# Pooled attention with a token and channel mixer: tail copies from SBUF, and the last tail maxima in the second bank of the AV result tile

## The chip, the cores and the metric

The kernel runs on one core of one Trainium2 chip. The metric is the device time of one execution in microseconds. Three timed runs of the kernel before gave 1417.49, 1419.48 and 1420.95 us; the median, 1419.48 us, is the figure to compare with. One further execution was profiled, and it took 1416.78 us; its trace spans 1414.8 us.

## The reference

For 8 batches and 8 heads, queries are pooled in pairs (1152 rows become 576), scored against 1152 keys, put through a softmax with its row maximum subtracted, and multiplied with the values. The result goes through a mixer: an angle, two token matrices, a channel matrix.

```python
q_pool = q.reshape(B, H, S // 2, 2, D).mean(axis=3)          # 8, 8, 576, 64
scores = np.matmul(q_pool, k.transpose(0, 1, 3, 2)) / np.sqrt(D)
scores = scores - np.max(scores, axis=-1, keepdims=True)
attn = np.exp(scores)
attn = attn / (np.sum(attn, axis=-1, keepdims=True) + 1e-09)
x = np.matmul(attn, v)                                       # -> 8, 576, 512
theta = x @ w_theta
zr, zi = x * np.cos(theta), x * np.sin(theta)
u = x + einsum('ts,bsd->btd', w_tok_r, zr) + einsum('ts,bsd->btd', w_tok_i, zi)
out = u + np.maximum(u @ w_ch, 0.0)
```

## The kernel before

The attention is the first stage (until about 932 us of the span), the mixer the second. The change lies in the first alone.

The unit of the attention is a **pair** of heads, numbered i = 0 to 31. The two heads lie in the two halves of the 128 partitions. For each pair, keys and pooled queries are turned by TensorE into a PSUM tile `pt` in two groups (g = 0: six key blocks; g = 1: six query blocks and three key blocks). ScalarE rounds each into the SBUF tile `hi` (L281), VectorE writes the remainder into `lo` (L292).

The **row maxima** of the scores are worked out ahead of the scores. 512 of a pair's 576 queries per head take 12 passes (`maxpass`, L305 on TensorE and L312 on VectorE). The last 64 queries of both heads, the *tail*, are packed by two ScalarE copies (`prep_tail`, L288) into one block-diagonal 128x128 tile, and `max_tail` multiplies it with all 1152 keys: 1024 of them into a tile `px` (L322, reduced by L331), the last 128 into a free corner of the `pt` of a later pair (L328, reduced by L332). The maxima of a pair are gathered into one row per head (`max_row`: a TensorE transpose into the tile `pmt`, copied by L344, sent by DMA) and enter the scores as a further matmul.

The **scores** of a pair are 18 steps (2 query halves u by 9 key blocks kt): eight matmuls into a tile `pe` (L371), one exponential on ScalarE into `pc` (L374), and a running sum on GpSimd (L383).

The **AV** product of a half u runs as one burst of 18 groups of matmuls, `av` (L392), into a tile `pa`, which ScalarE then copies out (L399). The rest of the work is put around the two bursts of a pair:

- the burst of u = 0 of pair i: `prep_all(i + 2, 1)`, then `max_row(i + 1)`, then `av(i, 0)`, then the sums of pair i - 1 (`norm_sum`, L408, in the `pmt` tile that L344 reads);
- the burst of u = 1 of pair i: `tail_prep(i)`, which turns group 0 of pair i + 3 and works out the tail maxima of pair i + 2, then `av(i, 1)`.

PSUM is used in **double tiles** of two banks (2 x 512 words per partition), in two rings of two: ring "e" holds `pe` and `pa`, ring "m" holds `pt`, `px`, `pmt` and `pm`. `pa` uses only columns 0 to 287 of its first bank. The order on every engine is written out by hand: each piece has a place on one scale of positions (`at`), the pieces are sorted by it, and each engine runs its instructions in just that order. Semaphore waits are put in between by a framework that follows which instruction writes and reads which tile.

Beside the attention, VectorE, ScalarE and GpSimd convert the mixer's weights piece by piece (L525 to L555).

Of the kernel before, what the change touches and what calls it, by code (L numbers as in the profile page):

```python
# [9 lines left out]
F32 = mybir.dt.float32  # L10
# [4 lines left out]
ALU = mybir.AluOpType  # L15
AX = mybir.AxisListType
# [75 lines left out]
def pooled_attention_moe_kernel(  # L92
# [11 lines left out]
    nc = tc.nc  # L104
    P = 128
    B, H, S, D = k.shape
    SQ = S // 2
    DM = H * D
    HALF = SQ // 2
    HT = SQ % P  # L110
# [3 lines left out]
    QP = SQ // QT  # L114
    NP = H // 2
    NPAIR = B * NP
# [31 lines left out]
    def bank2(kind, name):  # L148
        return psum["now"][0].tile([P, 2, 512], F32, tag=kind, name=name, bufs=PAIRS[kind])
# [38 lines left out]
    with ExitStack() as p1:  # L188
# [21 lines left out]
        state = {}  # L210
# [32 lines left out]
        def prep(i):  # L243
            st = state[i]
            for n in ("hi", "lo"):
                st[n] = opd.tile([P, SQ + S], F32R, tag=n, name=f"{n}{i}")
            st["nmr"] = nmrs[i % 2]

        K0 = {t: SQ * (t >= 6) + t * P for t in range(KT)}
        Q0 = 6 * P  # L250

        def prep_t(i, g):
            st = state[i]
            kn = st["kn"]
            pt = st["pt", g] = bank2("m", f"pt{g}_{i}")
            if g == 0:
                srcs = [[kn[:, t] for t in range(3 * n, 3 * n + 3)] for n in range(2)]
            else:
                qp = st["qp"]
                srcs = [[qp[:, t] for t in range(5)], [qp[:, 5]] + [kn[:, t] for t in (6, 7, 8)]]  # L260
            for n in range(2):
                c = 0
                for src in srcs[n]:
                    R = src.shape[0]
                    nc.tensor.transpose(  # L265
                        out=pt[:, n, c : c + R],
                        in_=src.rearrange("p h d -> p (h d)"),
                        identity=ident[0:R, 0:R],
                    )
                    c += R  # L270

        def prep_parts(i, g):
            st = state[i]
            c0, w = ((0, 3 * P), (Q0, 5 * QP))[g]
            return st["pt", g][:, :, 0:w], *(
                st[n][:, c0 : c0 + 2 * w].rearrange("p (b c) -> p b c", b=2) for n in ("hi", "lo")
            )

        def prep_hi(i, g):
            src, hi, lo = prep_parts(i, g)  # L280
            nc.scalar.copy(hi, src)  # L281

        def prep_tail(i):
            st = state[i]
            tl = st["tail"] = tails[i % 2]
            c = QP - HT
            for hs in HEADS:
                nc.scalar.copy(tl[hs, hs], st["pt", 1][hs, 1, c : c + HT])  # L288

        def prep_lo(i, g):  # L290
            src, hi, lo = prep_parts(i, g)
            nc.vector.tensor_tensor(lo, src, hi.bitcast(F32), ALU.subtract)  # L292
# [24 lines left out]
        def max_tail(i, pt):  # L317
            st = state[i]
            hi, tl, mx = st["hi"], st["tail"], st["mx"]
            pm = bank2("m", f"px{i}")  # L320
            for n, c, k, w in ((0, 0, 0, 4), (1, 0, 4, 2), (1, 2 * P, 6, 2)):
                nc.tensor.matmul(  # L322
                    pm[:, n, c : c + w * P], tl, hi[:, K0[k] : K0[k] + w * P], start=True, stop=True
                )
            st["pm", 0] = pm
            if pt is None:
                pt = bank2("m", f"py{i}")
            nc.tensor.matmul(  # L328
                pt[:, 0, 3 * P :], tl, hi[:, K0[8] : K0[8] + P], start=True, stop=True
            )  # L330
            nc.vector.tensor_reduce(mx[:, 8, 0:2], pm, AX.X, ALU.max)  # L331
            nc.vector.tensor_reduce(mx[:, 8, 2:3], pt[:, 0, 3 * P :], AX.X, ALU.max)  # L332

        def max_nm(i):
            st = state[i]
# [3 lines left out]
        def max_row(i):  # L339
            st = state[i]  # L340
            px = bank2("m", f"pmt{i}")
            nc.tensor.transpose(out=px[0:KT, 0, 0:P], in_=st["nm"], identity=ident)
            mT = st["mT"] = sml.tile([KT, P], F32R, tag="mT", name=f"mT{i}")
            nc.scalar.copy(mT, px[0:KT, 0, 0:P])  # L344
            return px
# [36 lines left out]
            first = st["pc"][u, 0] if kt == 1 else st["ss", u]  # L382
            nc.gpsimd.tensor_tensor(st["ss", u], first, st["pc"][u, kt], ALU.add)  # L383

        def av(i, u):
            st = state[i]
            if u == 0:
                st["xu"] = nrm.tile([P, 2, HALF], F32, tag="xu", name=f"xu{i}", bufs=3)
            pa = bank2("e", f"pa{i}_{u}")
            for kt in range(KT):  # L390
                for h, hs in enumerate(HEADS):
                    nc.tensor.matmul(  # L392
                        pa[hs, 0, 0:HALF],
                        st["vn"][:, h, kt, :],
                        st["pc"][u, kt][:, h, :],
                        start=(kt == 0),
                        stop=(kt == KT - 1),
                    )
            nc.scalar.copy(st["xu"][:, u, :], pa[:, 0, 0:HALF])  # L399

        def norm_sum(i, px):
            st = state[i]
            sets = [[st["ss", u]] + [st["pc"][u, kt] for kt in range(TAIL, KT)] for u in range(2)]
            for n in range(len(sets[0])):
                for h in range(2):
                    for u in range(2):
                        a = 32 * (2 * h + u)
                        nc.tensor.matmul(  # L408
                            px[a : a + 32, 1, 0:HALF],
                            ones,  # L410
                            sets[u][n][:, h, :],
                            start=(n == 0),
                            stop=(n == len(sets[0]) - 1),
                            tile_position=(0, a),
                        )
            sm = st["sm"] = sml.tile([P, HALF], F32, tag="sm", name=f"sm{i}", bufs=1)
            nc.scalar.activation(sm, px[:, 1, 0:HALF], AF.Identity, bias=eps)
# [38 lines left out]
        def burst(i, u):  # L456
            if u == 0:
                if i + 2 < NPAIR:
                    prep_all(i + 2, 1)
                px = max_row(i + 1) if i + 1 < NPAIR else bank2("m", f"pmt{i}")  # L460
                av(i, u)
                if i > 0:
                    norm_sum(i - 1, px)
            else:
                tail_prep(i)
                av(i, u)

        def prep_all(i, g):
            if g == 0:
                prep(i)  # L470
            prep_t(i, g)
            prep_hi(i, g)
            prep_lo(i, g)
            if g == 1:
                prep_tail(i)

        def tail_prep(i):
            more = i + 3 < NPAIR
            if more:
                prep(i + 3)  # L480
                prep_t(i + 3, 0)
            if i + 2 < NPAIR:
                max_tail(i + 2, state[i + 3]["pt", 0] if more else None)
            if more:
                prep_hi(i + 3, 0)
                prep_lo(i + 3, 0)

        def norm_store(i):
            b, hp = divmod(i, NP)
# [158 lines left out]
        def plan(i):  # L648
# [7 lines left out]
            if i < 2:  # L656
                at(PRO[i][1], 3, prep_all, i, 1)
                at(PRO[i][2], 3, max_tail, i, None)
# [12 lines left out]
            for u in range(2):  # L671
                at(base + AV_AT[u], 4, burst, i, u)
# [318 lines left out]
```

## Time and profile before

| | |
|---|---|
| timed runs, median | 1419.48 us (1417.49 to 1420.95, 3 runs) |
| profiled execution, own time | 1416.78 us |
| its span | 1414.8 us, mean granted TensorE clock 0.992 |
| busy share of the span | PE 96%, weight load 77%, GpSimd 64%, VectorE 61%, ScalarE 52% |
| DMA | 111.66 MB, 79 GB/s on average |

The profile's rows give, for an instruction, its start in us from the span's start, its length in us, engine, line, operation, output and inputs; in square brackets stands how long the engine was idle before it and what ended that. PE is TensorE's matmul, PEld its weight load, DVE VectorE, ACT ScalarE, POOL GpSimd. In the view of stretches, the column PEclk is the granted clock as a share of the full one, and the number behind an engine's busy time is its count of instructions.

### The profile page before, as it was taken

How to read it: one execution, taken by the hardware profiler on the slowest of the kernel's cores; microseconds unless marked ns; L12 is line 12 of the kernel's file. 1: busy time of each engine (PE TensorE's matmuls, PEld its weight loads, DVE VectorE, ACT ScalarE, POOL GpSimd, SP SyncE). 2: the span in 40 equal slices, each digit the busy share in tenths (PEclk: the TensorE clock that was granted, in tenths of full speed). 3: DMA queues.
4: the chain of work that ended last, by engine and by line, in shares of the span. 5: the costliest groups of instructions: out<-in, count | busy, mean ns of one | idle time of the engine just before them, and what ended most of it. 6: DMA issues, size and time to landing. Idle time of an engine off the chain costs nothing.

```text
span 1414.8 us, 29922 instructions
## 1 busy us (share of the span) xinstructions
PE 1352.8 (96%) x12178; PEld 1086.1 (77%) x12178; DVE 862.2 (61%) x1143; ACT 730.6 (52%) x1250; POOL 911.4 (64%) x672
## 2 busy tenths in 40 slices
PE   5999999999999999999999999999999999999998
PEld 4667676766676767767776766688999999999998
DVE  5866676777577767766687666355362553536442
ACT  2556465655555655556565655465444544445431
POOL 2789888978798889889898888834232413232210
PEclk7999999999999999999999999999999999999999
DMA  5224343434342443324343421231111211111111
GB/s 127 74 75 126 85 111 84 119 85 116 86 125 69 108 122 106 94 83 125 84 111 86 119 80 51 79 122 38 35 38 34 60 50 34 38 35 44 28 31 38
DMA packets 130906, 111.66 MB, mean 79 GB/s; under 512 B 95040, under 2 KB 95424, under 8 KB 130768
## 3 DMA queue, kind: packets, MB, share of 16 engines
q1 hardware_dynamic: 130592, 109.28, 28.0%
q8 instruction: 96, 1.57, 0.5%
q0 software_dynamic: 176, 0.46, 0.1%
q14 instruction: 42, 0.34, 0.1%
HBM read 88.29 MB, written 21.27 MB: 77 GB/s over the span
## 4 chain that ended last, share of the span: by engine, by line
PE 67%; DVE 15%; ACT 10%; DMA 3%; issue 3%; POOL 1%; SPq 0%; ACTq 0%; POOLq 0%; DVEq 0%
PE pa L392 16%; PE pe L371 16%; PE py L821 11%; PE pth L743 7%; PE pr L860 5%; DVE mx L312 5%; ACT pc L374 4%; PE pm L305 3%; PE pt L265 3%; PE pmt L408 2%; DMA kn<-in_k_dram 2%; DVE wf L532 1%; PE pxn L731 1%; DVE ws L530 1%; DVE lo L292 1%
## 5 line engine op out<-in xcount | busy, mean ns | idle before, releaser
L383 POOL TENSOR_TENSOR ss<-ss,pc 128x576 f32<-128x576 f32 x384 | 558.1, 1453 | 98.2 <-ACT pc L374 75.9
L312 DVE TENSOR_REDUCE mx<-pm 128x2 f32<-128x768 f32 x384 | 343.9, 950 | 134.8 <-PE pm L305 134.4
L374 ACT ACTIVATE pc<-pe 128x576 f32<-128x576 f32 x576 | 371.2, 652 | 102.2 <-PE pe L371 84.2
L392 PE MATMUL pa<-pc,vn 128*64 128x288 f32 x2304 | 293.5, 409 | 0.3 <-ACT pc L374 0.3
L794 POOL TENSOR_TENSOR Z<-ab,Z 128x512 fp32r<-128x512 f32 x40 | 52.2, 1305 | 306.0 <-ACT Z L790 277.8
L392 PEld LDWEIGHTS pa<-pc,vn 128*64 128x64 f32 x2304 | 159.7, 137 | 110.7 <-ACT pc L374 4.8
L821 PE MATMUL py<-wtk,Z 128*128 128x288 f32 x1728 | 241.7, 297 | 0.0
L821 PEld LDWEIGHTS py<-wtk,Z 128*128 128x128 f32 x1728 | 233.2, 189 | 1.3
L371 PE MATMUL pe<-hi 64*128 64x288 f32 x1152 | 203.1, 349 | 14.9 <-ACT pc L374 6.5
L371 PEld LDWEIGHTS pe<-hi 64*128 64x128 f32 x1152 | 108.3, 184 | 92.9 <-ACT pc L374 57.9
L371 PE MATMUL pe<-hi,lo 64*128 64x288 f32 x1152 | 170.8, 293 | 0.0
L371 PE MATMUL pe<-lo,hi 64*128 64x288 f32 x1152 | 170.8, 293 | 0.0
L371 PE MATMUL pe<-nmr,oner 64*128 64x288 f32 x1152 | 169.5, 290 | 0.0
L305 PE MATMUL pm<-hi 64*128 64x384 f32 x768 | 138.1, 359 | 14.6 <-DVE mx L312 8.6
L371 PEld LDWEIGHTS pe<-lo,hi 64*128 64x128 f32 x1152 | 109.8, 187 | 0.0
L371 PEld LDWEIGHTS pe<-hi,lo 64*128 64x128 f32 x1152 | 109.1, 186 | 0.0
L371 PEld LDWEIGHTS pe<-nmr,oner 64*128 64x128 f32 x1152 | 109.0, 185 | 0.0
L292 DVE TENSOR_TENSOR lo<-pt,hi 128x768 fp32r<-128x768 f32 x64 | 67.6, 1057 | 66.9 <-ACT hi L281 66.9
L860 PEld LDWEIGHTS pr<-us,wch 128*128 128x128 f32 x768 | 104.5, 188 | 2.0
L860 PE MATMUL pr<-us,wch 128*128 128x288 f32 x768 | 105.8, 295 | 0.0
L281 ACT CAST hi<-pt 128x768 fp32r<-128x768 f32 x64 | 56.2, 878 | 91.5 <-DVE mx L332 74.3
L383 POOL TENSOR_TENSOR ss<-pc,pc 128x576 f32<-128x576 f32 x64 | 93.8, 1466 | 3.0 <-ACT pc L374 3.0
(105 smaller groups left out, 1652.7 us busy)
## 6 DMA issues: line engine op xcount, KB each, us to landing
qn<-in_q_dram SPq DMA_DIRECT2D x32, 576.0 KB
kn<-in_k_dram SPq DMA_DIRECT2D x64, 288.0 KB
vn<-in_v_dram SPq DMA_DIRECT2D x32, 576.0 KB
dn<-ro SPq DMA_DIRECT2D x64, 144.0 KB
xd<-xu SPq DMA_DIRECT2D x32, 288.0 KB
xT<-xd SPq DMA_DIRECT2D x8, 1152.0 KB
out_dram<-on SPq DMA_DIRECT2D x23, 192.0 KB
out_dram<-on SPq DMA_DIRECT2D x23, 128.0 KB
```

Of the source, the lines that this page charges most:

```text
L281: nc.scalar.copy(hi, src)
L292: nc.vector.tensor_tensor(lo, src, hi.bitcast(F32), ALU.subtract)
L305: nc.tensor.matmul(pm[:, h, 0:W], hi[hs, Q0 + j * P : Q0 + (j + 1) * P], hi[hs, K0[3 * g] : K0[3 * g] + W], start=True, stop=True,)
L312: nc.vector.tensor_reduce(mx[:, j : j + 5 : 4, g : g + 1], pm[:, :, 0:W], AX.X, ALU.max)
L371: nc.tensor.matmul(pe[:, h, 0:HALF], w[hs], x[hs], start=(n == 0), stop=(n == 3))
L374: nc.scalar.activation(pcs[u, kt], pe[:, :, 0:HALF], AF.Exp, scale=SC)
L383: nc.gpsimd.tensor_tensor(st["ss", u], first, st["pc"][u, kt], ALU.add)
L392: nc.tensor.matmul(pa[hs, 0, 0:HALF], st["vn"][:, h, kt, :], st["pc"][u, kt][:, h, :], start=(kt == 0), stop=(kt == KT - 1),)
L743: nc.tensor.matmul(th, xs[c][:, j * P : (j + 1) * P], ws[:, c], start=(n == 0), stop=(n == 11))
L794: engine("zlo", b).tensor_tensor(Z[1], t, Z[0].bitcast(F32), ALU.subtract)
L821: nc.tensor.matmul(st["py", c, u][:, 0:HALF], Z[zi][:, c * P : (c + 1) * P], wtk[wi][:, kw, u * HALF : (u + 1) * HALF], start=(i == 0 and ...
L860: nc.tensor.matmul(pr[u][:, 0:HALF], wch[wi][:, c, e * P : (e + 1) * P], st["us", ui][:, c, u * HALF : (u + 1) * HALF], start=(n == 0), st ...
```

## The change

It has two parts. `prep_tail` copies the 64 tail queries from the rounded tile `hi` in SBUF and no longer from `pt` in PSUM. `max_tail` writes the last 128 columns of the tail scores into the second bank of the tile it is given, at column 0, and in a burst of u = 1 that tile is no longer `pt` but the `pa` of the burst, which `tail_prep` now takes from ring "e" and hands to `av`. With `pt` no longer shared, its rounding and remainder are written before the tail maxima.

```diff
         def prep_tail(i):
...
-            c = QP - HT
+            c = Q0 + SQ - HT
             for hs in HEADS:
-                nc.scalar.copy(tl[hs, hs], st["pt", 1][hs, 1, c : c + HT])
+                nc.scalar.copy(tl[hs, hs], st["hi"][hs, c : c + HT].bitcast(F32))
...
             nc.tensor.matmul(
-                pt[:, 0, 3 * P :], tl, hi[:, K0[8] : K0[8] + P], start=True, stop=True
+                pt[:, 1, 0:P], tl, hi[:, K0[8] : K0[8] + P], start=True, stop=True
             )
             nc.vector.tensor_reduce(mx[:, 8, 0:2], pm, AX.X, ALU.max)
-            nc.vector.tensor_reduce(mx[:, 8, 2:3], pt[:, 0, 3 * P :], AX.X, ALU.max)
+            nc.vector.tensor_reduce(mx[:, 8, 2:3], pt[:, 1, 0:P], AX.X, ALU.max)
...
-        def av(i, u):
+        def av(i, u, pa=None):
...
-            pa = bank2("e", f"pa{i}_{u}")
+            if pa is None:
+                pa = bank2("e", f"pa{i}_{u}")
...
             else:
-                tail_prep(i)
-                av(i, u)
+                av(i, u, tail_prep(i))
...
         def tail_prep(i):
-            more = i + 3 < NPAIR
-            if more:
-                prep(i + 3)
-                prep_t(i + 3, 0)
+            if i + 3 < NPAIR:
+                prep_all(i + 3, 0)
+            pa = bank2("e", f"pa{i}_1")
             if i + 2 < NPAIR:
-                max_tail(i + 2, state[i + 3]["pt", 0] if more else None)
-            if more:
-                prep_hi(i + 3, 0)
-                prep_lo(i + 3, 0)
+                max_tail(i + 2, pa)
+            return pa
```

The order of the instructions shows what this moves. The rows are those around two bursts of pair 16; a name is the tile's with its pair, its half or group, and a running number, and in square brackets stands whose semaphore an instruction waits for. (Line numbers past L389 are one higher after the change: L392 becomes L393, and so on.)

On TensorE, the burst of u = 1 before:

```order
L265 MATMUL pt0_19_6888<-ident_63,kn19_6739 128x128 x5
L322 MATMUL px18_6895<-hi18_6498,tail_0_112 128x512 [waits DVE_49]
L322 MATMUL px18_6895<-hi18_6498,tail_0_112 128x256 x2
L328 MATMUL pt0_19_6888<-hi18_6498,tail_0_112 128x128
L392 MATMUL pa16_1_6904<-pc16_10_6652,vn16_6365 64x288 [waits Activation_49]
L392 MATMUL pa16_1_6904<-pc16_10_6652,vn16_6365 64x288
```

and after the change:

```order
L265 MATMUL pt0_19_6888<-ident_63,kn19_6739 128x128 x5
L322 MATMUL px18_6898<-hi18_6498,tail_0_112 128x512 [waits DVE_49]
L322 MATMUL px18_6898<-hi18_6498,tail_0_112 128x256 x2
L328 MATMUL pa16_1_6897<-hi18_6498,tail_0_112 128x128 [waits Activation_49]
L393 MATMUL pa16_1_6897<-pc16_10_6652,vn16_6365 64x288 [waits DVE_49]
L393 MATMUL pa16_1_6897<-pc16_10_6652,vn16_6365 64x288
```

The matmuls stand in the same order. The wait for ScalarE (the ring's buffer is free) moved one matmul ahead, to L328, and the first AV matmul now waits for VectorE: for the count that L332 raises when it has read this same `pa16_1`. This stands so in the bursts of pairs 0 to 29.

On VectorE, the same burst before:

```order
L312 TENSOR_REDUCE mx18_6757<-pm18_12_6851 128x2 [waits PE_49]
L331 TENSOR_REDUCE mx18_6757<-px18_6895 128x2 [waits PE_49]
L332 TENSOR_REDUCE mx18_6757<-pt0_19_6888 128x1 [waits PE_49]
L292 TENSOR_TENSOR lo19_6887<-pt0_19_6888,hi19_6886 128x768 [waits Activation_49]
L432 RECIPROCAL rc15_6762<-rc15_6762 128x9 [waits DMAHW3_49]
```

and after the change:

```order
L312 TENSOR_REDUCE mx18_6757<-pm18_12_6851 128x2 [waits PE_49]
L292 TENSOR_TENSOR lo19_6887<-pt0_19_6888,hi19_6886 128x768 [waits Activation_49]
L331 TENSOR_REDUCE mx18_6757<-px18_6898 128x2 [waits PE_49]
L332 TENSOR_REDUCE mx18_6757<-pa16_1_6897 128x1 [waits PE_49]
L433 RECIPROCAL rc15_6762<-rc15_6762 128x9 [waits DMAHW3_49]
```

The remainder L292 moved ahead of the two reduces.

On ScalarE, the burst of u = 0 before:

```order
L281 CAST hi18_6498<-pt1_18_6682 128x960 [waits PE_49]
L288 CAST tail_0_112<-pt1_18_6682 64x64 [waits DVE_49]
L288 CAST tail_0_112<-pt1_18_6682 64x64
L344 CAST mT17_6698<-pmt17_6696 9x128 [waits DMAHW6_49,DMAHW0_49,PE_49]
L399 COPY xu16_6700<-pa16_0_6701 128x288 [waits DMAHW0_49,PE_49]
```

and after the change:

```order
L281 CAST hi18_6498<-pt1_18_6682 128x960 [waits PE_49]
L288 CAST tail_0_112<-hi18_6498 64x64 [waits Activation_49]
L288 CAST tail_0_112<-hi18_6498 64x64
L344 CAST mT17_6698<-pmt17_6696 9x128 [waits DMAHW6_49,DMAHW0_49,PE_49]
L400 COPY xu16_6700<-pa16_0_6701 128x288 [waits DMAHW0_49,PE_49]
```

The tail copies stand where they stood. They waited for VectorE's remainder L292 on the same `pt`, and now wait for ScalarE's own rounding, the instruction ahead of them.

## The prediction

> **What bounds the kernel now.** I read the page first, then the stretches, then the timeline around the two bursts of a pair, then the view of waits. The rows of the page and two stretches of the attention:
>
> ```profile
> span 1414.8 us, 29922 instructions
> PE 1352.8 (96%) x12178; PEld 1086.1 (77%) x12178; DVE 862.2 (61%) x1143; ACT 730.6 (52%) x1250; POOL 911.4 (64%) x672
> 75.00:500.00 425.00, 406.23 (x4202) 293.78 (x4200) 295.40 (x348) 240.79 (x417) 362.77 (x266) 1.00 0.37 99
> 500.00:865.00 365.00, 355.28 (x3689) 258.69 (x3687) 260.84 (x309) 212.47 (x367) 316.46 (x230) 1.00 0.37 101
> ```
>
> Over 790 us of attention TensorE's matmuls are busy for 761.5, at full clock: 28.5 us idle in all, a microsecond per pair. TensorE sets the time, and whatever makes it wait is paid in full; taking waits from other engines pays only where TensorE stood behind them. The burst of u = 1 of pair 16, in order of time:
>
> ```profile
> 506.93 0.87 PE L265 MATMUL pt<-ident,kn 128*128 128x128 f32 x6
> 507.29 0.66 ACT L374 ACTIVATE pc<-pe 128x576 f32<-128x576 f32 x1
> 507.56 0.71 PE L322 MATMUL px<-hi,tail 128*128 128x512 f32 x3
> 508.11 0.22 PE L328 MATMUL pt<-hi,tail 128*128 128x128 f32 x1
> 508.26 4.59 PE L392 MATMUL pa<-pc,vn 128*64 128x288 f32 x36
> 508.31 1.23 DVE L331 TENSOR_REDUCE mx<-px 128x2 f32<-128x1024 f32 x1 [1.61 <-PE px L322]
> 509.45 0.28 DVE L332 TENSOR_REDUCE mx<-pt 128x1 f32<-128x128 f32 x1
> 509.77 0.80 ACT L281 CAST hi<-pt 128x768 fp32r<-128x768 f32 x1 [1.82 <-DVE mx L332]
> 510.60 0.96 DVE L292 TENSOR_TENSOR lo<-pt,hi 128x768 fp32r<-128x768 f32 x1 [0.87 <-ACT hi L281]
> 511.47 0.21 DVE L432 RECIPROCAL rc<-rc 128x9 f32<-128x9 f32 x1
> 512.89 0.40 ACT L399 COPY xu<-pa 128x288 f32<-128x288 f32 x1 [2.33 <-PE pa L392]
> ```
>
> TensorE goes from the tail matmul into 4.59 us of AV without a stop. The two reduces, the rounding and the remainder all run beneath the AV and end at 511.56, 1.3 us before it does.
>
> **The change part by part.**
>
> *The new wait of the AV.* After the change the first AV matmul waits for L332, and L332 now stands behind the rounding, the remainder and L331, none of which can start before the transposes are done. Worked out on these rows: the rounding starts when the exponential ends, 507.29 + 0.66 = 507.95, and lasts 0.80; the remainder starts 0.03 later, at 508.79 (509.77 + 0.80 to 510.60 gives that step); the next VectorE instruction starts 0.87 after it (510.60 to 511.47), so L331 at 509.66; from there to the end of L332 are 1.42 (508.31 to 509.45 + 0.28); a TensorE matmul starts about 0.05 after the reduce it waits for. The AV starts at 511.14 instead of 508.26: 2.9 us of idle TensorE in this burst. Where the exponential ended before the transposes did, the same sum gives 2.8. What is late next is the copy L399 and the next scores, by the same 2.9; nothing catches it up, since TensorE had no slack.
>
> The order of the change has this wait in 30 bursts. 29 of them have the rounding and the remainder. In how many VectorE is free in time shows here: the first row groups all 32 pairs, the others are the first and the last of 11 late bursts and, third, the worst.
>
> ```profile
> DVE mx L331 <- PE px L322: 28.0, 19, 2.6
> 59.66 0.71 PE L392 MATMUL pa<-pc,vn 128*64 128x288 f32 x4
> 61.00 1.21 DVE L331 TENSOR_REDUCE mx<-px 128x2 f32<-128x1024 f32 x1
> 621.55 0.43 DVE L525 TENSOR_SCALAR raw<-raw 128x512 uint32<-128x512 uint32 x1 [3.89 <-DMA raw<-in_moe_w_theta_dram]
> 621.89 1.22 DVE L331 TENSOR_REDUCE mx<-px 128x2 f32<-128x1024 f32 x1
> 812.25 0.71 PE L392 MATMUL pa<-pc,vn 128*64 128x288 f32 x4
> 813.88 1.21 DVE L331 TENSOR_REDUCE mx<-px 128x2 f32<-128x1024 f32 x1
> ```
>
> In 19 pairs VectorE waited for TensorE before L331 (18 of the 29 bursts and one of the prologue). In the other 11 it was late with a weight conversion, and L331 started 1.34 (first), 1.63 (last) and on average 1.40 us after the AV instead of 0.05. So far this cost nothing; now the lateness is added to TensorE's stall: 1.40 + 0.03 + 0.87 + 1.42 + 0.06 = 3.8 us. Sum: 18 x 2.78 + 11 x 3.78 = 91.6, and 2.4 for the burst of pair 29 (late, without rounding), 94 us. Bounds: 30 x 2.7 = 81 if the lateness goes away (a pair that lasts longer gives VectorE and the loads time), and 105 if it doubles.
>
> *Rounding and remainder earlier.* ScalarE's idle time before L281 goes away, and the buffer of `pt` comes free about 1.8 us sooner. ScalarE then waits 2.33 us for the AV all the same, so this by itself is worth nothing; the cover is the AV.
>
> *The tail copies.* In the burst of u = 0 they no longer wait for the remainder, and the copy L344 behind them is earlier.
>
> ```profile
> ACT hi L281 <- DVE mx L332: 74.3, 29, 4.6
> ACT tail L288 <- DVE lo L292: 53.7, 32, 4.5
> PE pmt L408 <- ACT mT L344: 3.8, 6, 1.6
> PE pm L305 <- DVE mx L312: 8.6, 21, 1.3
> 496.34 0.43 ACT L288 CAST tail<-pt 64x64 fp32r<-64x64 f32 x2 [1.23 <-DVE lo L292]
> 496.79 0.26 ACT L344 CAST mT<-pmt 9x128 fp32r<-9x128 f32 x1
> 498.67 0.69 PE L408 MATMUL pmt<-ss,ones 128*32 128x288 f32 x8
> ```
>
> Mostly L344 was done 1.6 us before TensorE came to L408 (497.05 against 498.67), so most of the 53.7 us was hidden. Six times TensorE did wait, 3.8 us in all: gained, -4. The copies' new wait for ScalarE's own rounding, which this trace has nowhere, lies between nothing and the 0.43 us of both copies per pair; beneath 1.6 us of slack it costs nothing. SBUF instead of PSUM as source changes 2 x 0.21 us under the same cover.
>
> *VectorE's state after the stall.* While TensorE stands, VectorE finishes what it did beneath the AV, and then has 4.5 us for its weight work. The waits of L305 for L312, 8.6 us, some 6 of them past the prologue and mostly 8 us after a late burst, should shrink: -5 (bounds 0 and -6).
>
> Nothing changes in number on any queue: no DMA is added, and one PSUM tile less is taken in pair 29. The sum so far: 1416.8 + 94 - 4 - 5 = 1502 for a profiled execution.
>
> *The clock.* No idle stretch of TensorE after the prologue was longer than 1.64 us; the new ones are 2.8 to 5. The rows show what the clock does with sparse windows. It changes only at steps of a grid of 3.41 us, and these are stretches of that grid:
>
> ```profile
> 10.67:14.07 3.40, 1.09 (x9) 0.62 (x10) 2.62 (x4) 1.37 (x3) 1.96 (x2) 1.00 0.54 122
> 14.08:17.49 3.41, 2.40 (x10) 1.02 (x10) 3.41 (x5) 0.00 (x0) 0.00 (x0) 0.50 0.90 218
> 31.15:34.55 3.40, 3.40 (x28) 3.28 (x27) 2.44 (x4) 1.89 (x3) 1.55 (x2) 0.50 1.11 303
> 34.57:37.97 3.40, 2.14 (x16) 1.49 (x14) 2.54 (x4) 0.65 (x1) 2.65 (x2) 1.00 0.97 284
> 382.72:386.12 3.40, 1.76 (x20) 0.83 (x20) 2.56 (x4) 0.96 (x4) 0.46 (x1) 1.00 0.00 0
> 1410.14:1413.54 3.40, 0.00 (x0) 0.00 (x0) 0.00 (x0) 0.00 (x0) 0.00 (x0) 1.00 0.77 222
> 1413.55:1414.70 1.15, 0.00 (x0) 0.00 (x0) 0.00 (x0) 0.00 (x0) 0.00 (x0) 0.50 0.00 0
> 30.09 0.44 PE L371 MATMUL pe<-lo,hi 64*128 64x288 f32 x2
> 30.34 0.44 PE L371 MATMUL pe<-hi,lo 64*128 64x288 f32 x2
> 513.02 0.30 PE L371 MATMUL pe<-lo,hi 64*128 64x288 f32 x2
> 513.15 0.29 PE L371 MATMUL pe<-hi,lo 64*128 64x288 f32 x2
> ```
>
> After a window with 2.31 us idle, and after one idle throughout, the clock fell to a half; after one with 1.64 idle it stayed; it came back after a window full of matmuls. So somewhere between 1.64 and 2.31 us of idle in one window it falls; I take the middle, 1.98. A stall of S < 3.41 at a random place on the grid leaves more than that in one window with a chance of (3.41 + S - 2 x 1.98) / 3.41: 0.66 at 2.8, and near 0.95 for the late ones. That makes 18 x 0.66 + 11 x 0.95 + 0.5 = 23 falls (17 by the one bound, 27 by the other). The AV behind is dense, so each lasts one window. At the half clock a pair of matmuls follows after 0.25 us and not 0.13, so a window loses up to 1.6 us, some 1.45 where the stall reaches into it: 33 us (25 to 40). The sum is 1502 + 33 = 1535. The profiled execution lies 2.7 us under the median of the timed runs; I leave the figure there.
>
> The Trainium skill's page "TensorE: Matmul & The Clock Gate", section "Part 1: The HAM clock gate", has the clock fall only after an idle window of about 3.4 us. By that rule these stalls would make one or two falls at most and the sum stay at 1502 to 1505; the trace's row at 10.67, with matmuls in it, speaks against it, which is why it stands as a rival with less than half the chance.
>
> **The rivals.**
>
> *The stall without the clock*: the clock falls only after a window with no matmul at all, as at 1410.14. For it speaks that row; against it the one at 10.67, though that lies in the prologue. Stalls over 3.41 us are about eight and seldom cover a whole window: one fall, 1504.
>
> *The clock stays down longer*: the prologue held the half clock for six windows, from 14.08 on, with windows only partly busy. If a stall's remainder keeps the next window from counting as full, a fall lasts two windows: 1502 + 2 x 33 = 1568. Against it: by then 4.6 us of AV at the full rate, nearly 9 at the half one, fill the window.
>
> *The wait is met in time*: `pa`'s columns 0 to 287 and the new 128 columns lie in different banks, and if the AV did not in fact stand behind L332, TensorE would keep its pace and the gains alone be left: 1416.8 - 4 - 5 = 1408. It decides where L332 ends before L328 does, 508.33 in the burst above; it ends at 511.1 by rows of which none is optional. The skill's page "PSUM — Partial Sum Buffer", section "PSUM bank collisions raise a hardware error", asks for a guard by bank and quadrant of partitions alone, so by it this wait isn't needed; the order of the change has the wait all the same.
>
> **How the numbers follow.** The stall with the clock at half for a window each: 0.56, 1520 to 1548. The stall alone: 0.28, 1495 to 1510. The longer half clock: 0.10, around 1568. Something between the first two: 0.03. The wait met in time: 0.02; unforeseen, 0.01. The predicted time is that of the first, 1535. The range has to take in the first two: from 1496 to 1556, which leaves out most of the third and the last two. Faster by over 0.2% (what a measurement of this kernel can tell from no change) is 0.02, within it 0.01, slower 0.97.
>
> **What would show it.** Right: idle TensorE before the AV's line, released by L332, in 30 bursts, 2.7 us at the least and about 94 in all; the order rounding, remainder, L331, L332 beneath that gap; ScalarE's waits at L281 for L332 and at L288 for L292 gone, and TensorE's at L408 for L344 too; PEclk under 1.00 in stretches behind the bursts of u = 1. The first step is wrong if the AV begins before L332 has ended; the clock step if the mean granted clock stays at 0.99. The forecast would also miss if the late bursts are no longer late (down to 1525) or if weight conversions shift further under the new pace.

## The result and the profile after

The changed kernel took 1546.49 us (median of 4 runs, 1545.62 to 1549.01) against 1420.22 us for the kernel before (4 runs): a ratio of 1.0904, 95% interval 1.0887 to 1.0920. Its profiled execution took 1549.01 us, 132.2 more than that of before. The page of the changed kernel, with the span, the busy times and the granted clock in 40 slices:

```profile
span 1547.0 us, 29878 instructions
PE 1404.5 (91%) x12178; PEld 1105.7 (71%) x12178; DVE 856.8 (55%) x1143; ACT 734.2 (47%) x1250; POOL 911.3 (59%) x672
PEclk7999999998999988999989999999999999999999
```

TensorE ran the same 12178 matmuls, but was busy 51.7 us longer (1352.8 before) and idle 142.5 us (62.0 before). The burst of u = 1 of pair 16, the one shown before:

```profile
509.06 0.87 PE L265 MATMUL pt<-ident,kn 128*128 128x128 f32 x6
510.24 0.22 PE L328 MATMUL pa<-hi,tail 128*128 128x128 f32 x1
510.81 0.96 DVE L292 TENSOR_TENSOR lo<-pt,hi 128x768 fp32r<-128x768 f32 x1 [1.96 <-ACT hi L281]
511.68 1.22 DVE L331 TENSOR_REDUCE mx<-px 128x2 f32<-128x1024 f32 x1
512.81 0.28 DVE L332 TENSOR_REDUCE mx<-pa 128x1 f32<-128x128 f32 x1
513.15 4.14 PE L393 MATMUL pa<-pc,vn 128*64 128x288 f32 x20 [2.69 <-DVE mx L332]
```

Remainder, large reduce and small reduce follow each other on VectorE at the steps read from the trace of before, and TensorE stands 2.69 us until L332 has ended. From there the first 20 AV matmuls take 4.14 us, where 36 took 4.59 before. Summed over the whole execution, the kernel before had these waits for keys and this line of the AV (busy time, mean of one in ns, idle time before):

```profile
PE pt L265 <- DMA kn<-in_k_dram: 12.4, 8, 7.7
L392 PE MATMUL pa<-pc,vn 128*64 128x288 f32 x2304 | 293.5, 409 | 0.3 <-ACT pc L374 0.3
```

and after the change, first the waits, then the AV's line:

```profile
PE pa L393 <- DVE mx L332: 92.1, 30, 4.9
PE pm L305 <- DVE mx L312: 8.5, 18, 1.3
PE pt L265 <- DMA kn<-in_k_dram: 7.9, 1, 7.9
L393 PE MATMUL pa<-pc,vn 128*64 128x288 f32 x2304 | 343.1, 459 | 92.4 <-DVE mx L332 92.1 <-ACT pc L374 0.3
```

The new wait stands in 30 bursts and costs 92.1 us. The AV's line grew from 293.5 us to 343.1, 49.6 of the 51.7 us that TensorE was busy longer. The waits at L408 for L344 (3.8 us) are gone, those for the keys fell from 12.4 to 7.9 (the one at the start of the kernel is left), and those of L305 for L312 stayed (8.6 before). The whole account of the profiled execution: 92.4 of idle before the AV, 51.7 of slower matmuls, and 11.9 less idle elsewhere (142.5 - 92.4 = 50.1 against 62.0), 132.2.

Where the clock stood at a half, on the grid of 3.41 us (busy times by engine, TensorE's first, then PEclk). A window is one step of this grid, a fall the step from the full clock to the half:

```profile
512.80:516.20 3.40, 3.05 (x14) 1.59 (x16) 0.41 (x3) 0.00 (x0) 3.32 (x3) 0.50 0.08 6
639.09:642.50 3.41, 1.76 (x14) 1.24 (x10) 2.02 (x4) 1.57 (x4) 3.34 (x4) 1.00 0.57 166
642.51:645.91 3.40, 2.12 (x10) 1.15 (x12) 1.35 (x3) 0.00 (x0) 2.75 (x2) 0.50 0.03 1
738.08:741.48 3.40, 1.65 (x16) 1.30 (x12) 1.38 (x3) 2.02 (x4) 3.40 (x4) 1.00 0.02 1
837.10:840.50 3.40, 2.69 (x12) 1.47 (x14) 0.78 (x3) 0.00 (x0) 3.40 (x4) 0.50 0.03 1
157.78:161.18 3.40, 2.73 (x12) 1.48 (x14) 1.22 (x3) 0.00 (x0) 3.14 (x3) 0.50 0.36 113
```

The first row is the window in which the AV of pair 16 began: half clock. The records of the clock have 25 such falls in the attention, 16 of one window and 9 of two, 34 windows or 116 us in all. The second row is the busiest window that was followed by a fall (third row: the half clock behind it), the fourth the emptiest that was not: between 1.65 and 1.76 us busy, about half of a window, either happened. The last two are half-clock windows at the edge of recovery: after the one with 2.69 us busy the clock stayed down, after the one with 2.73 it rose.

### The profile page after: what moved, and what is told of

The parts are those of the page before. It is cut to its first block, busy times and chain, and to the rows that moved or that the text cites. A ratio compares the mean times of both kernels' runs of the same rounds, so it can differ in the third digit from the quotient of the medians.

```text
span 1547.0 us, 29878 instructions
## 1 busy us (share of the span) xinstructions
PE 1404.5 (91%) x12178; PEld 1105.7 (71%) x12178; DVE 856.8 (55%) x1143; ACT 734.2 (47%) x1250; POOL 911.3 (59%) x672
## 4 chain that ended last, share of the span: by engine, by line
PE 68%; DVE 16%; ACT 9%; issue 3%; POOL 2%; DMA 1%; SPq 0%; ACTq 0%; POOLq 0%; DVEq 0%
PE pa L393 21%; PE pe L371 15%; PE py L818 10%; PE pth L740 6%; PE pr L857 5%; DVE mx L312 5%; ACT pc L374 4%; PE pm L305 3%; PE pt L265 3%; DVE mx L331 2%; PE pmt L409 2%; DVE lo L292 2%; ACT hi L281 1%; POOL ss L383 1%; PE pxn L728 1%
## 5 line engine op out<-in xcount | busy, mean ns | idle before, releaser
L312 DVE TENSOR_REDUCE mx<-pm 128x2 f32<-128x768 f32 x384 | 344.0, 951 | 288.1 <-PE pm L305 287.9
L393 PE MATMUL pa<-pc,vn 128*64 128x288 f32 x2304 | 343.1, 459 | 92.4 <-DVE mx L332 92.1
L374 ACT ACTIVATE pc<-pe 128x576 f32<-128x576 f32 x576 | 372.5, 652 | 99.4 <-PE pe L371 81.7
L393 PEld LDWEIGHTS pa<-pc,vn 128*64 128x64 f32 x2304 | 179.6, 155 | 234.6 <-DVE mx L332 96.5
L371 PE MATMUL pe<-hi 64*128 64x288 f32 x1152 | 205.6, 353 | 12.2 <-ACT pc L374 5.5
L400 ACT COPY xu<-pa 128x288 f32<-128x288 f32 x64 | 25.6, 400 | 367.5 <-PE pa L393 367.5
L371 PEld LDWEIGHTS pe<-hi 64*128 64x128 f32 x1152 | 108.4, 184 | 92.1 <-ACT pc L374 52.7
L371 PE MATMUL pe<-hi,lo 64*128 64x288 f32 x1152 | 171.1, 293 | 0.0
L371 PE MATMUL pe<-lo,hi 64*128 64x288 f32 x1152 | 171.0, 293 | 0.0
L371 PE MATMUL pe<-nmr,oner 64*128 64x288 f32 x1152 | 169.9, 291 | 0.0
L305 PE MATMUL pm<-hi 64*128 64x384 f32 x768 | 137.5, 357 | 14.2 <-DVE mx L312 8.5
L371 PEld LDWEIGHTS pe<-lo,hi 64*128 64x128 f32 x1152 | 109.8, 187 | 0.0
L371 PEld LDWEIGHTS pe<-hi,lo 64*128 64x128 f32 x1152 | 109.3, 186 | 0.0
L371 PEld LDWEIGHTS pe<-nmr,oner 64*128 64x128 f32 x1152 | 109.1, 185 | 0.0
L292 DVE TENSOR_TENSOR lo<-pt,hi 128x768 fp32r<-128x768 f32 x64 | 67.5, 1054 | 71.5 <-ACT hi L281 71.5
```

The costliest lines, as they stand in the source:

```text
L305: nc.tensor.matmul(pm[:, h, 0:W], hi[hs, Q0 + j * P : Q0 + (j + 1) * P], hi[hs, K0[3 * g] : K0[3 * g] + W], start=True, stop=True,)
L312: nc.vector.tensor_reduce(mx[:, j : j + 5 : 4, g : g + 1], pm[:, :, 0:W], AX.X, ALU.max)
L371: nc.tensor.matmul(pe[:, h, 0:HALF], w[hs], x[hs], start=(n == 0), stop=(n == 3))
L374: nc.scalar.activation(pcs[u, kt], pe[:, :, 0:HALF], AF.Exp, scale=SC)
L393: nc.tensor.matmul(pa[hs, 0, 0:HALF], st["vn"][:, h, kt, :], st["pc"][u, kt][:, h, :], start=(kt == 0), stop=(kt == KT - 1),)
```

## The experiments

The theory after the result: two costs, the wait of the AV for VectorE's chain (92 us) and the half clock that these gaps bring (52 us), less a gain of some 12 us that has nothing to do with the shared tile. The main rival: the AV itself is slower because its tile is shared with a reader on VectorE.

**e1, the gap filled.** In the changed kernel 18 matmuls that nobody reads (`fill` is 18) are set between L328 and the AV.

```diff
+            for _ in range(fill):
+                nc.tensor.matmul(
+                    pt[:, 0, HALF:], tl, hi[:, Q0 : Q0 + 512 - HALF], start=True, stop=True
+                )
```

> Theory (stall plus clock): the AV still begins only after L332, so its wait stays: some 92 us from the tail matmul to the first AV matmul over 30 bursts. But 18 added matmuls, written into unread columns of the AV tile's first bank, keep TensorE busy for about 2.2 us of each, so few windows have over 1.7 us idle: at most 5 falls of the clock in place of 25, the AV's lines back at about 0.13 us a matmul, and the time falls by 40 to 50 us to 1495 to 1508 although work is added. Rival (the clock is not what costs: the longer AV comes from VectorE reading the second bank of the tile, or of a neighbouring one, while TensorE writes the first): 1545 or more. The fillers' results are never read.

Measured: 1506.82 us, ratio 1.0629 (1.0605 to 1.0654), 40 us under the change with 540 matmuls more. Its busy times, its wait, and the lines of the AV and of the added matmuls:

```profile
PE 1419.7 (94%) x12718; PEld 1145.9 (76%) x12718; DVE 860.5 (57%) x1143; ACT 734.1 (49%) x1250; POOL 911.6 (61%) x672
PE pa L398 <- DVE mx L337: 30.1, 30, 3.1
L398 PE MATMUL pa<-pc,vn 128*64 128x288 f32 x2304 | 298.3, 414 | 30.4 <-DVE mx L337 30.1 <-ACT pc L379 0.3
L333 PE MATMUL pa<-hi,tail 128*128 128x224 f32 x540 | 66.5, 277 | 0.0
```

The gap before the AV is still 30.1 + 66.5 = 96.6 us long, now mostly filled; the clock fell three times instead of 25, and the AV's line is back at 298.3 us, within 5 of the kernel before (293.5), though its tile is shared as in the change. The rival falls: the 50 us were the clock.

**e2, the tail ahead of the rounding.** The tail maxima stand where they stood before the change, but still write the AV's tile.

```diff
+                prep_t(i + 3, 0)
+            pa = bank2("e", f"pa{i}_1")
+            if i + 2 < NPAIR:
+                max_tail(i + 2, pa)
+            if more:
+                prep_hi(i + 3, 0)
+                prep_lo(i + 3, 0)
```

> The tail maxima again stand ahead of the rounding and the remainder, still in the AV's tile. Theory: the AV waits for L331 and L332 alone, 1.5 us in the 18 bursts where VectorE is on time and about 2.9 in the 11 late ones, 62 us in all in place of 92; 1.5 us of idle is too little for the clock, so falls only come from the late bursts, some 9, costing about 2 us each: 1420 + 62 + 18 - 10 = 1490 (1475 to 1505). Rival (order does not matter, the AV pays for the shared tile): as the change, 1546.

Measured: 1484.46 us, ratio 1.0473 (1.0445 to 1.0501), with 8 falls of one window each.

**e3, the small reduce first.** The last 128 columns are multiplied before the other 1024 and reduced before rounding, remainder and the large reduce (`between` writes the rounding and the remainder of pair i + 3).

```diff
+            nc.tensor.matmul(
+                pt[:, 1, 0:P], tl, hi[:, K0[8] : K0[8] + P], start=True, stop=True
+            )
             pm = bank2("m", f"px{i}")
...
+            nc.vector.tensor_reduce(mx[:, 8, 2:3], pt[:, 1, 0:P], AX.X, ALU.max)
+            if between is not None:
+                between()
+            nc.vector.tensor_reduce(mx[:, 8, 0:2], pm, AX.X, ALU.max)
```

> The last 128 tail columns are multiplied first and reduced first (both into and from the AV's tile), then rounding, remainder and the large reduce. Theory: L332 ends beneath the three other tail matmuls, so the 18 bursts on time have a stall of at most 0.2 us; the 11 late ones keep VectorE's lateness, 1.75 us on average, some 20 us in all, with one to four falls of the clock: 1420 + 23 + 4 - 10 = 1437 (1425 to 1450). Rival (any reader of the AV's tile on VectorE holds the AV by the whole chain): 1490 or more.

Measured: 1431.39 us, ratio 1.0094 (1.0072 to 1.0117), two falls. The waits of the AV, of e2 and of e3 (where the small reduce has the line L331 and the AV L395):

```profile
PE pa L393 <- DVE mx L332: 60.7, 30, 4.1
```

```profile
PE pa L395 <- DVE mx L331: 20.1, 12, 2.9
```

92.1, 60.7 and 20.1 us, with 34, 8 and 2 windows at half clock: the AV waits for that part of VectorE's chain that stands before the small reduce, and the times follow. In e3 only 12 waits are left, as many as there were bursts with VectorE late in the kernel before (the 11, and that of pair 29).

**e4, the weight conversions later.** The change, with the three conversion steps of positions 18.0 to 19.25 moved behind the burst.

```diff
-W_AT = (9.45, 9.5, 9.85, 10.5, 12.75, 18.0, 18.6, 19.25, 20.45)
+W_AT = (9.45, 9.5, 9.85, 10.5, 12.75, 19.26, 19.27, 19.28, 20.45)
```

> The change with the weight conversions of positions 18.0 to 19.25 moved to just behind the burst of u = 1. Theory: VectorE is on time in nearly all 30 bursts, each stall is 2.8 us, 85 us in place of 92; falls of the clock stay frequent (2.8 us still leaves over 1.7 in a window 8 times in 10), so 1546 - 7 - 4 = 1535 (1525 to 1542). Rival (lateness is only shifted, or conversions behind the burst make TensorE wait for VectorE at L305): 1546 or more.

Measured: 1518.97 us, ratio 1.0709 (1.0684 to 1.0734): 27.5 under the change, where 11 were expected. TensorE's busy time and wait, then the two neighbouring windows over which one gap lies, then a window that holds another gap:

```profile
PE 1388.0 (91%) x12178; PEld 1098.4 (72%) x12178; DVE 854.1 (56%) x1143; ACT 733.3 (48%) x1250; POOL 909.1 (60%) x672
PE pa L393 <- DVE mx L332: 80.2, 30, 3.5
687.85:691.25 3.40, 2.48 (x26) 1.99 (x22) 1.46 (x3) 2.40 (x4) 3.34 (x4) 1.00 0.49 155
691.27:694.67 3.40, 1.66 (x14) 1.06 (x16) 3.40 (x5) 0.00 (x0) 3.32 (x3) 1.00 0.01 2
186.19:189.59 3.40, 0.72 (x8) 0.47 (x8) 2.41 (x4) 0.69 (x1) 3.40 (x5) 1.00 0.00 0
```

The wait fell by 12 us, where 7 were expected (lateness is gone from nearly all bursts), and the matmuls got 16.5 us shorter, where 4 were: 16 falls in place of 25, where 8 in 10 of 30 had been reckoned. Nearly every gap has the same 2.69 us here; in the first two rows one is cut by the grid into 0.9 and 1.7 us and the clock stays up, in the third one lies in one window and it falls behind it. How often a gap is cut like that had been reckoned as chance, at 2 in 10; in this run 14 of 30 gaps brought no fall, and whether that is chance or comes from the pace of the pairs is not shown.

**e5, the tail copies alone.** The kernel before with the first part of the change.

```diff
-            c = QP - HT
+            c = Q0 + SQ - HT
...
-                nc.scalar.copy(tl[hs, hs], st["pt", 1][hs, 1, c : c + HT])
+                nc.scalar.copy(tl[hs, hs], st["hi"][hs, c : c + HT].bitcast(F32))
```

> Only the first part of the change: the tail copies read the rounded queries in SBUF, everything else as before. Theory: ScalarE's 54 us of waiting for the remainder go away, but TensorE stood behind them only at L408, 3.8 us in six pairs: 1418 - 4 = 1414, ratio 0.996 to 0.999, and TensorE's wait at L408 for L344 gone. Rival (ScalarE's waiting is hidden altogether): 1.000. Rival (the copies' new wait for ScalarE's own rounding costs): 1.002 or more.

Measured: 1404.29 us, ratio 0.9897 (0.9882 to 0.9912), a gain of 14.7 us where 4 were expected. The wait at L408 is gone, as expected. What else became faster stands in the waits of this run (those for keys, not those of L305), and its cause in the timeline of the kernel before around one late burst (SPq is the queue that issues DMAs):

```profile
PE pm L305 <- DVE mx L312: 9.8, 23, 1.5
PE pt L265 <- DMA kn<-in_k_dram: 8.1, 2, 7.8
```

```profile
442.44 0.43 ACT L288 CAST tail<-pt 64x64 fp32r<-64x64 f32 x2 [3.90 <-DVE lo L292]
442.89 0.26 ACT L344 CAST mT<-pmt 9x128 fp32r<-9x128 f32 x1
443.17 0.64 SPq L351 DMA_DIRECT2D nmr<-mT  x1
446.46 1.41 SPq L226 DMA_DIRECT2D kn<-in_k_dram  x2
452.25 0.74 PE L265 MATMUL pt<-ident,kn 128*128 128x128 f32 x5 [0.44 <-DMA kn<-in_k_dram]
```

The tail copies waited 3.90 us for the remainder, L344 behind them was late, so was the sending of the row (L351), and the key loads stand behind it in the same queue: the next transposes on TensorE then wait for keys. There are seven such waits in the kernel before, 4.7 us in all, and one of 0.3 in e5.

**e6, the corner of pt kept.** As e5, and rounding and remainder ahead of the two tail reduces as in the change; the last 128 columns stay in `pt`, so the AV needs nothing from VectorE (`between` as in e3).

```diff
             nc.tensor.matmul(
                 pt[:, 0, 3 * P :], tl, hi[:, K0[8] : K0[8] + P], start=True, stop=True
             )
+            if between is not None:
+                between()
             nc.vector.tensor_reduce(mx[:, 8, 0:2], pm, AX.X, ALU.max)
```

> The first part of the change, and rounding and remainder ahead of the two tail reduces as in the change, but the last 128 tail columns stay in the corner of pt. Theory: the AV waits for nothing on VectorE, so the order that the change has on VectorE costs nothing by itself: 1412 to 1418, within 0.3% of the run with the copies alone. Rival (the new order delays VectorE, for the remainder waits for the rounding): 0.3% or more above it.

Measured: 1405.13 us, ratio 0.9904 (0.9890 to 0.9917), under the 1412 to 1418 expected, as e5 is, but the same as e5: the order on VectorE costs nothing unless the AV waits for it. From this kernel to the change it is the place of these 128 columns that differs, in `pt` or in the `pa` that is taken early for them: 1405.13 against 1546.49 us.

**e7 and e8, late bursts removed.** e3 and e5, each with the edit of e4.

> The kernel in which L332's reduce comes first, with the weight conversions moved behind the burst. Theory: the 20 us of stall that were left there came from VectorE's lateness; it goes, the clock stays up, and what is left is the gain of the shared tile and the copies: 1431 - 18 - 4 = 1409 (1405 to 1415), under the kernel before. Rival (the conversions then make TensorE wait elsewhere): 1420 or more.

> The copies alone, with the weight conversions moved behind the burst; the AV has no wait for VectorE. Theory: lateness costs only where L305 waits for L312, some 6 us, so 1408 to 1414, no more than 0.4% under the copies alone; if it equals the run with L332 first and the conversions moved, sharing the AV's tile brings nothing even when its wait is hidden. Rival: no difference to the copies alone.

Measured: 1412.14 us (0.9949, 0.9937 to 0.9962) and 1411.30 us (0.9952, 0.9939 to 0.9964). With the small reduce first and VectorE on time, the shared tile costs nothing and brings nothing. Moving the conversions cost e5 7 us, against the expectation. TensorE's waits at L305 for VectorE add up to 17.0 us in the trace of e8 and to 13.8 in that of e5, and one of 1.3 at L408 is back: about the 4.5 us by which the two profiled executions differ. What the medians differ by beyond that stays open.

**e9, the row ahead of the tail copies.** The kernel before with `prep_tail` moved behind `max_row` in the burst of u = 0; the copies read PSUM as before.

```diff
                 px = max_row(i + 1) if i + 1 < NPAIR else bank2("m", f"pmt{i}")
+                if i + 2 < NPAIR:
+                    prep_tail(i + 2)
...
-            if g == 1:
-                prep_tail(i)
```

> The kernel before with one thing moved: on ScalarE the copy L344 of the maxima's row stands ahead of the two tail copies, which still read PSUM and still wait for the remainder. Theory (the copies alone gained because L344 came earlier: for TensorE at L408, and for the key loads queued on SP behind the sending of that row): the same gain as the copies alone, 1405 to 1409, with the waits for the keys down from 12.4 to about 8 us and those at L408 gone. Rival (the gain is from the source in SBUF, or from ScalarE's other work behind the tail copies coming earlier): under half of it, 1412 or more.

Measured: 1408.21 us, ratio 0.9928 (0.9916 to 0.9940): 10.4 us of gain with no change of the copies' source. ScalarE still waits for the remainder, and TensorE no longer for the row or, past the prologue, the keys:

```profile
ACT tail L288 <- DVE lo L292: 49.6, 32, 4.6
PE pt L265 <- DMA kn<-in_k_dram: 7.7, 1, 7.7
```

The waits that went, 4.7 us for keys and 3.8 at L408, are 8.5 of the 9.3 us by which the profiled execution (1407.46) lies under that of before.

**e10 and e11, the keys first.** `load_k` from -43.2 to -43.6 sets the key loads ahead of the row in the queue: e10 is the kernel before with it, e11 is e5 with it.

```diff
-    "load_k": -43.2,
+    "load_k": -43.6,
```

> The kernel before with the key loads set ahead of the sending of the maxima's row in SP's queue, nothing else. Theory: TensorE's waits for the keys past the prologue, some 4.5 us, go and those at L408 stay: 1419 - 4 to 6 = 1413 to 1415. Rival (the keys are late for another reason): 1418 or more.

> The copies alone and the key loads first. Theory: both remove the same waits for the keys, so little is left to add: 1402 to 1405, within 0.2% of the copies alone. Rival (the two gains add up): 1400 or less.

Measured: e10 1416.53 us (0.9984, 0.9975 to 0.9992), e11 1409.00 us (0.9937, 0.9924 to 0.9949). Waits of e10, then one of e11:

```profile
PE pt L265 <- DMA kn<-in_k_dram: 7.8, 1, 7.8
PE pmt L408 <- ACT mT L344: 4.1, 6, 2.0
PE pe L371 <- DMA nmr<-mT: 2.3, 1, 2.3
```

```profile
PE pe L371 <- DMA nmr<-mT: 3.0, 1, 3.0
```

The waits for keys past the prologue are gone in both, as said; e10 gained 2.1 us, less than the 4 to 6 expected, and e11 lost 5 to e5. Both misses lie mostly at the start. The edit also moves the first pairs' loads, and at 33 us TensorE now waits once for the row, 2.3 us in e10 and 3.0 in e11, a wait that neither the kernel before nor e5 has. The first AV matmul starts at 49.15 us in e10 against 46.54 before, and at 49.82 in e11 against 46.09 in e5. From there on e10's trace is 5.0 us shorter than that of before, as expected, and e11's 1.0 longer than that of e5.

## Why the prediction was right

**The new wait, right.** 30 bursts, 94 us said, 92.1 measured, and its parts came out too: mostly 2.69 us in the 18 bursts on time against 2.8, 3.8 on average in the 11 late ones against 3.8, and 2.3 in that of pair 29 against 2.4. The steps of the chain came out as read from one burst; e2 and e3 took parts of it away and got 60.7 and 20.1 us, against 62 and 20 expected beforehand.

**The clock, right in kind, too small in size.** 33 us said, with bounds of 25 and 40; 51.7 measured. The number of falls was right (25 against 23), and so was the loss of a window (51.7 / 34 = 1.5 us). The mis-sized term is the length: each fall was to last one window, and 9 of 25 lasted two. The prediction gave the longer half clock a chance of 0.10 as an all-or-nothing case and held against it that the AV fills the next window. It does so only if the gap ended early enough: where its remainder reaches more than about 0.7 us into the next window, that one is busy under 2.7 of 3.41 us, and the clock stays down for another. So it was in all nine. The nine extra windows, 14 us, and two more falls make most of the 18.7 us missed. The point between 1.64 and 2.31 us of idle lay at about 1.7, near its lower bound. The sum of the three terms fell short of the profiled execution by 14.2 us (18.7 here, less 1.6 on the wait and 2.9 on the gains), so the other two misses, small and the other way, hid some of this one.

**The gains, right in sum, wrong in part.** 9 us said, 11.9 measured. L408 gave its 3.8. The 5 us of L305's waiting for VectorE did not come (8.6 to 8.5): that VectorE is ahead after a stall does not reach those waits. In their place came 4.5 us of waits for keys, which the prediction had not followed: it stopped at L344 and did not ask what stands behind the row in SP's queue. The other 3.6 us are spread over smaller waits, the largest part 1.0 at L371 for L374 (6.5 to 5.5). So the sum came out near by luck, one term in place of another. The tail copies were sized at 4 us and are worth 14.7 (e5). Of these, 10.4 come with L344's place (e9); what the other 4 are is open, and no trace shows them: the profiled execution of e5, at 1407.59 us, is as long as that of e9, while its other three took 1404.15 to 1404.34. The copies' new wait cost nothing. In the timeline of e5 they begin 0.03 us after the rounding has ended (488.06, after 487.07 + 0.96):

```profile
487.07 0.96 ACT L281 CAST hi<-pt 128x960 fp32r<-128x960 f32 x1 [0.26 <-PE pt L265]
488.06 0.50 ACT L288 CAST tail<-hi 64x64 fp32r<-64x64 f32 x2
488.58 0.25 ACT L344 CAST mT<-pmt 9x128 fp32r<-9x128 f32 x1
```

**The rivals.** The clock fell after windows with up to 1.76 us of matmuls in them, so the rival without it, at 1504, is out. Out with it is the Trainium skill's rule (page "TensorE: Matmul & The Clock Gate", section "Part 1: The HAM clock gate") read as a window that is wholly idle; the trace agrees with its window of 3.41 us and with the two values of the clock. The wait met in time did not happen: the AV waited in all 30 bursts.

**The best version.** e5, the first part of the change without the second, at 1404.29 us (0.9897), beats both kernels; e6 is equal to it.

## What to carry to other kernels

Before a PSUM tile with a free bank is lent to another product, look at who reads that product and what stands ahead of the reader on its engine: in this kernel the wait is on the whole tile, and the owner's matmuls stood behind all that VectorE had to do before the reader. A gap on TensorE has two prices, its length and the clock behind it; filling gaps of 3 us with matmuls that nobody reads brought 40 us here, though the gaps themselves stayed and the kernel was still 6% slower than the one before. When a copy comes earlier, follow it into the DMA queue that it feeds: loads that have nothing to do with it may stand behind it.

## What the runs showed of the hardware

Two thresholds of the clock, in windows of 3.41 us. At full clock it fell when a window was busy less than about half: in the change after 1.76 us and less, with 1.65 as the emptiest window without a fall. The edge is not sharp, for in other runs the clock stayed up after windows of less, down to 1.46 us (e10). At half clock it rose again only when a window was busy about 0.8 of its length (stayed down at 2.69 us, rose at 2.73). A gap of 2.69 us that lies across two windows can go unpunished, and the five of e4 that lay in one window each brought a fall; so by the 1.5 us that a window of half clock cost, I estimate the same gap at 2.7, 4.2 or 5.7 us.
